# An attention and mixture-of-experts kernel: the second expert's rows turned in two halves, and the router's search step issued in two parts

## The chip, the cores and the metric

The kernel runs on one core of a Trainium2 chip. A core has five engines that run their own instruction queues in order: TensorE (PE, with its weight loads shown as PEld), VectorE (DVE), ScalarE (ACT), GpSimd (POOL) and SyncE (SP, here used to start DMAs). The metric is the device time in microseconds (us) of one execution.

## What is computed

Attention with a sigmoid in place of the softmax, for 8 batches and 12 heads of 448 positions and 64 columns; its result, as 3584 rows of 768 columns, goes through a mixture of 8 experts, each of which takes 448 rows:

```
scores = scale * q @ k.T - log(S)
attn = 1 / (1 + exp(-scores))
x = (attn @ v), heads side by side          # (3584, 768)
logits = x @ w_gate                          # (3584, 8)
for idx in argsort(-logits.flatten()):       # best pair of token and expert first
    tok, e = idx // E, idx % E
    if assigned[tok] >= 0 or counts[e] >= cap: continue
    assigned[tok] = e; counts[e] += 1
for e in range(E):
    h = maximum(x[assigned == e] @ w1[e], 0)
    out[assigned == e] = h @ w2[e]
```

All inputs and the output are float32. An expert's sequence of work follows from the order in which experts fill up.

## The kernel before

**Attention** runs first, pair of heads by pair of heads, and stores the rows to a scratch tensor (xs). The change does not touch it.

**The experts** follow, in the order in which they fill up, kx = 0 to 7. What the text calls expert 1 is the one with kx = 1, the second. In each, first products (`moe`, L718 to L739) give hidden columns in four groups of 256, then second products (L752 to L777) give output columns in three groups of 256. Each float32 matrix is split into a high and a low part (wh and wl, xh and xl, hh and hl), so a product is three matmuls: L734, L736, L738, then L771, L773, L775. The text calls each such matmul of 128x128 by 448 columns one product. There are 4 x 2 x 2 x 9 = 144 and 3 x 2 x 2 x 12 = 144 of them in an expert, 288 in all. Expert 0 does its first group in two cuts of 256 and 192 columns, which makes 324. The generator `moe` yields once per product.

**Rows of an expert.** Its 448 rows come in four blocks j of 128, 128, 128 and 64. `gather` (L623) fetches one block from xs with an indirect DMA on POOL's queue. `xturn` (L628) turns one half hf (384 of 768 columns) of a block: three transposes on PE into a bank of PSUM (L639), from which ACT writes xh (L642) and DVE writes xl (L643). So an expert needs eight of these turnings. The bank is one of two named tp, or, for `wide` and the second half, half of one of two tiles named sc. The sc tiles also take the sums of the products. The first products read the half hf = 0 (dd = 0 to 2) in their first 18 products of a group and hf = 1 in the next 18.

**Turning back.** `untranspose` (L648) turns an expert's output back, on PE (L652) through a tp bank and ACT (L657), and after the third group `scatter` sends a block of rows out on POOL's queue.

**Weights.** `stream` loads the weights (wr, on SP's queue, after the expert's number r_ei has been read) and splits them three and two units ahead: ACT writes wh (L603), POOL writes wl (L605).

**The router** finds the next expert and its rows. It is a generator (`phase`, L324). For each expert from 1 to 6 it does `keys`, a search of 16 steps, `pick`, `place` and `lists`, and ends with the list of rows, r_idx (L298). A step of the search counts on DVE how many keys lie over three thresholds (L178, three passes), and then, for every expert but the first, sums the counts and sets the next thresholds on DVE too (L194 to L217). `yield T_...` hands back a planned cost in ns.

**The order** of all this is written out by the loop at L816 to L858, instruction for instruction: the schedule is manual, and each engine takes its instructions in that order. The loop keeps a clock of planned time. Each product adds 189 ns (107 in expert 0's first group). At each product it may issue the next part of the router, if the clock has reached the time set by the previous part, and one of the `chores`: a list of jobs with due times, of which the first one due is taken, not more than one in 1000 ns:

```
if t >= t_route:
    t_route = t + next(route, 0) + SLACK
...
if t >= t_chore:
    c = next((c for c in chores if c[0] <= t), None)
    if c:
        ...
        t_chore = t + CHORE_NS
```

`prepare` (L820) is called when the list of the next expert is there: it makes the gathers and the eight turnings of that expert chores (for expert 1 the gathers are issued at once), the turnings due 5000 to 14000 ns later. `flush` (L833), at an expert's end, issues whatever chores the next expert cannot do without. Ahead of the first product the router is run through expert 0's list, and then by one part more (EARLY).

Of the kernel before, what the change touches and what calls it, by code (L numbers as in the profile page):

```python
# [26 lines left out]
YT_BUFS = 3  # L27
LATE_PER_STEP = 3
LATE_KEYS = 7
T_KEYS, T_KE, T_STEP, T_DVE, T_KAP, T_PICK, T_TOT, T_OH, T_BT = 3600, 2100, 2050, 2025, 500, 2600, 600, 3800, 600  # L30
SLACK = 150
CHORE_NS = 1000
H_POOL = 8
# [10 lines left out]
def _s32(v):  # L44
    v &= 0xFFFFFFFF
    return v - (1 << 32) if v >= (1 << 31) else v
# [72 lines left out]
class Router:  # L119
# [42 lines left out]
    def search(self, pe):  # L162

        nc, K, wk, KT = self.nc, self.K, self.wk, self.KT
        p = self.bank()
        for g in range(2):
            nc.tensor.transpose(p[:, g * 112:(g + 1) * 112],
                                KT[:, g].rearrange("p e c -> p (e c)"), K.ident[:112, :112])
        KE = wk.tile([128, 224], F32, name="r_KE")
        nc.vector.tensor_copy(KE, p[:, :224])  # L170
        T, JP = K.c0, None
        X = None if pe else self.bank().bitcast(I32)
        for st in range(16):
            sh = 30 - 2 * st
            cnt = wk.tile([128, 3], BF, name="r_cnt") if pe else K.CN
            for i in range(3):
                junk = wk.tile([128, 224], BF, name="r_junk")
                nc.vector.tensor_scalar(junk, KE, T[:, i:i + 1].bitcast(F32), None, OP.is_ge, OP.add,  # L178
                                        accum_out=cnt[:, i:i + 1])
            nX = None  # L180
            if 0 < st < 15:
                nX = wk.tile([128, 3], I32, name="r_X") if pe else X[:, 4 * (st % 2):4 * (st % 2) + 3]
            acc = wk.tile([128, 1], F32, name="r_acc")
            j2 = wk.tile([128, 3], F32, name="r_j2")
            if pe:
                if nX is not None:
                    nc.vector.tensor_scalar(nX, K.kk[:, st + 1], JP, None, OP.bitwise_xor)
                yield T_STEP
                pc = self.bank()
                nc.tensor.matmul(pc[:, :3], K.G, cnt, start=True, stop=True)  # L190
                tot = pc[:, :3]
            else:
                ct = wk.tile([128, 32], F32, name="r_ct")
                nc.vector.transpose(ct, cnt)  # L194
                if nX is not None:
                    nc.vector.tensor_scalar(nX, K.kk[:, st + 1], JP, None, OP.bitwise_xor)
                s2 = wk.tile([128, 2], F32, name="r_s2")
                nc.vector.tensor_reduce(s2, ct.rearrange("p (e r) -> p e r", r=16), AX.X, OP.add)
                ct2 = wk.tile([128, 32], F32, name="r_ct")
                nc.vector.transpose(ct2.rearrange("p (e r) -> p e r", r=16), s2[:, :, None].to_broadcast([128, 2, 16]))  # L200
                tot = ct2[:, :3]
            nc.vector.tensor_scalar(j2, tot, 447.5, TWO23, OP.is_ge, OP.add, accum_out=acc)
            nJ = wk.tile([128, 1], I32, name="r_J")
            if st == 0:
                J = wk.tile([128, 1], I32, name="r_J0")
                nc.vector.tensor_scalar(J, acc.bitcast(I32), sh, None, OP.logical_shift_left)
                PF = wk.tile([128, 1], I32, name="r_PF")
                nc.vector.tensor_scalar(PF, J, 31, -1, OP.arith_shift_right, OP.bitwise_xor)
                nc.vector.tensor_scalar(nJ, PF, _s32(0x80000000), J, OP.bitwise_or, OP.bitwise_xor)
                T = wk.tile([128, 3], I32, name="r_T")  # L210
                nc.vector.tensor_scalar(T, K.kk[:, 1], nJ, None, OP.bitwise_xor)
            else:
                if st < 15:
                    T = wk.tile([128, 3], I32, name="r_T")
                    nc.vector.scalar_tensor_tensor(T, acc.bitcast(I32).to_broadcast([128, 3]), sh, nX,
                                                   OP.logical_shift_left, OP.bitwise_xor)
                nc.vector.tensor_scalar(nJ, acc.bitcast(I32), sh, JP, OP.logical_shift_left, OP.bitwise_xor)  # L217
            JP = nJ
            if not pe:
                yield T_DVE  # L220
        kap = wk.tile([128, 1], I32, name="r_kap")
        nc.vector.tensor_scalar(kap, JP, K.gfin, None, OP.bitwise_xor)
        self.kap = kap.bitcast(F32)
# [116 lines left out]
def moe_attention(tc, q, k, v, w_gate, w1, w2, out):  # L340
# [7 lines left out]
    with contextlib.ExitStack() as ctx:  # L348
# [270 lines left out]
        def blocks():  # L619
            for j in range(4):  # L620
                yield j, min(128, S - 128 * j)

        def gather(kx, j, n):  # L623
            t = xg[kx, j] = xp.tile([128, DM], F32, name="xr", bufs=XR_BUFS)
            nc.gpsimd.indirect_dma_start(out=t[:n], out_offset=None, in_=xs,  # L625
                                         in_offset=bass.IndirectOffsetOnAxis(ap=listed[kx][:n, j:j + 1], axis=0))

        def xturn(kx, j, n, hf, wide):  # L628
            if (j, hf) == (0, 0):
                XH[kx] = (xp.tile([128, ND, S], F32R, name="xh", bufs=2),  # L630
                          xp.tile([128, ND, S], F32R, name="xl", bufs=2))
            xh, xl = XH[kx]
            if wide and hf:
                p = ps_s.tile([128, 2, 512], F32, name="sc")[:, 0]
            else:
                p = ps_t.tile([128, 512], F32, name="tp")
            for i in range(3):
                dd = hf * 3 + i
                nc.tensor.transpose(p[:, i * n:(i + 1) * n], xg[kx, j][:n, dd * 128:(dd + 1) * 128], ident[:n, :n])  # L639
            pv = p[:, :3 * n].rearrange("p (a t) -> p a t", a=3)  # L640
            sl = (slice(None), slice(hf * 3, hf * 3 + 3), slice(j * 128, j * 128 + n))
            nc.scalar.activation(xh[sl], pv, AF.Copy)  # L642
            nc.vector.tensor_tensor(xl[sl], pv, xh[sl].bitcast(F32), OP.subtract)  # L643

        scat, chores = [], []
        MM = 189

        def untranspose(kx, yr, i, yt, j, n, t0=0, end=False):  # L648
# [167 lines left out]
        for kx in range(E):  # L816
            turned = kx + 1 == E
            start = clock[0]

            def prepare():  # L820
                t0 = clock[0]
                lag = max(5000, min(14000, start + 40000 - t0))
                for j, n in blocks():
                    if kx:
                        chores.append((t0 + 1500 * j, kx + 1, lambda j=j, n=n: gather(kx + 1, j, n)))
                    else:
                        gather(1, j, n)
                for j, n in blocks():
                    for hf in range(2):
                        chores.append((t0 + lag + 1500 * j, kx + 1,  # L830
                                       lambda j=j, n=n, hf=hf: xturn(kx + 1, j, n, hf, False)))

            def flush(kx):  # L833
                for c in [c for c in chores if c[1] <= kx]:
                    chores.remove(c)
                    c[2]()

            for step, cost in enumerate(moe(kx)):
                clock[0] += cost
                t = clock[0]  # L840
                if kx == 0 and step == 35:
                    flush(0)
                if t >= t_route:
                    t_route = t + next(route, 0) + SLACK
                if not turned and kx + 1 in listed:
                    prepare()
                    turned = True
# [3 lines that stand above are left out]
                        chores.remove(c)  # L851
                        c[2]()
                        t_chore = t + CHORE_NS
            if not turned:
                while kx + 1 not in listed:
                    next(route)
                prepare()
            flush(kx + 1)  # L858
# [28 lines left out]
```

## Time and profile before

| | us |
|---|---|
| median of 3 runs | 883.03 (881.66 to 885.39) |
| the profiled execution | 883.43 |
| its span, first to last instruction | 881.7 |
| PE busy within the span | 840.1 |
| DVE busy | 542.4 |
| first product of expert 0 | at 332.80 |
| first product of expert 1 | at 405.83 |
| first product of expert 2 | at 475.69 |

Rows of the profile read like this. In a timeline: start, duration, engine, line of the kernel, operation, output and input tiles by name, shape, count, and in brackets how long the engine was idle before and for whom it waited. In a table of windows: the window, its length, then the busy time of each engine asked for (with the number of instructions), the clock that was granted to PE as a share of full speed, the busy share of the DMA engines, and GB/s. A matmul's recorded duration reaches into the next one's, since matmuls are pipelined; the distance of starts is what one costs.

### The profile page before, as it was taken

The numbers are of one execution on the slowest core, as the hardware profiler recorded it, in microseconds if no ns is written. First come the engines' busy times: TensorE is split into PE (matmuls) and PEld (weight loads), VectorE is DVE, ScalarE is ACT, GpSimd is POOL, SyncE is SP. The second block draws the span as 40 slices with busy tenths as digits, with TensorE's granted clock in tenths as the row PEclk, the third lists the DMA queues.
The fourth block names the chain that finished last, engine by engine and source line by source line (L and its number), as shares of the span: only waits on it lengthen the run. The fifth ranks groups of instructions, "written<-read, shape, count | busy, mean of one in ns | idle before, by whom it ended". The sixth has DMA issues, their size and how long they took to land.

```text
span 881.7 us, 16211 instructions
## 1 busy us (share of the span) xinstructions
PE 840.1 (95%) x5467; PEld 636.9 (72%) x5467; DVE 542.4 (62%) x2060; ACT 447.3 (51%) x612; POOL 466.0 (53%) x446
## 2 busy tenths in 40 slices
PE   6999999999999739998999999999999999999996
PEld 3455555555554528987988988988888888999996
DVE  4566555555554988958859879779779631332130
ACT  6777677777775734434434434534434344541420
POOL 9744344444410014854864873873883883851561
PEclk9999999999999979998999999999999999999999
DMA  9866766666621855443442442551542542634643
GB/s 173 165 142 149 153 126 127 127 126 127 126 43 54 270 192 154 120 138 123 128 136 97 160 155 81 177 162 57 189 153 72 170 153 90 209 96 141 203 151 126
DMA packets 213811, 122.16 MB, mean 139 GB/s; under 512 B 153344, under 2 KB 202496, under 8 KB 213728
## 3 DMA queue, kind: packets, MB, share of 16 engines
q1 hardware_dynamic: 200992, 87.62, 38.2%
q0 software_dynamic: 10880, 33.28, 12.0%
q8 instruction: 43, 0.70, 0.3%
q10 hardware_dynamic: 1856, 0.23, 0.2%
q14 instruction: 40, 0.33, 0.1%
HBM read 96.76 MB, written 24.31 MB: 137 GB/s over the span
## 4 chain that ended last, share of the span: by engine, by line
PE 82%; DVE 11%; issue 2%; DMA 2%; POOL 1%; SPq 1%; ACT 1%; POOLq 0%; DVEq 0%; ACTq 0%
PE tp L457 13%; PE sc L433 11%; PE sc L736 9%; PE sc L734 9%; PE sc L738 9%; PE sc L773 6%; PE sc L775 6%; PE sc L771 6%; DVE r_junk L178 4%; PE tp L463 2%; PE sc L443 2%; PE tp L639 2%; PE tp L652 2%; PE tp L478 1%; PE rt L289 1%
## 5 line engine op out<-in xcount | busy, mean ns | idle before, releaser
L605 POOL TENSOR_TENSOR wl<-wr,wh 128x768 fp32r<-128x768 f32 (+1 forms) x96 | 204.9, 2145 | 124.5 <-ACT wh L603 116.8
L423 ACT ACTIVATE at<-sc,bias 128x896 f32<-128x896 f32 x168 | 161.5, 1006 | 67.1 <-PE sc L443 38.4
L383 POOL DMA_DIRECT2D nkq<-in_q_dram x188 | 118.4, 646 | 116.2 <-DVE kqT L408 104.6
L775 PE MATMUL sc<-hh,wl 128*128 128x448 f32 (+2 forms) x400 | 150.2, 375 | 0.0
L738 PE MATMUL sc<-xh,wl 128*128 128x448 f32 (+2 forms) x396 | 146.2, 369 | 0.0
L736 PE MATMUL sc<-xl,wh 128*128 128x448 f32 (+2 forms) x396 | 146.0, 369 | 0.1
L773 PE MATMUL sc<-hl,wh 128*128 128x448 f32 (+2 forms) x400 | 145.5, 364 | 0.2 <-POOL hl L746 0.2
L734 PE MATMUL sc<-xh,wh 128*128 128x448 f32 (+2 forms) x396 | 145.0, 366 | 0.0
L771 PE MATMUL sc<-hh,wh 128*128 128x448 f32 (+2 forms) x400 | 144.1, 360 | 0.4 <-issue 0.4
L178 DVE TENSOR_SCALAR_CACHE_REDUCE r_junk<-r_KE,r_T 128x224 bf16<-128x224 f32 x315 | 123.2, 441 | 0.1
L603 ACT ACTIVATE wh<-wr 128x768 fp32r<-128x768 f32 (+1 forms) x112 | 102.0, 939 | 36.3 <-DMA wr<-in_moe_w_dram 23.4
L457 PE MATMUL tp<-at,nv 128*64 128x448 f32 x576 | 118.8, 548 | 0.0
L746 POOL TENSOR_TENSOR hl<-yt,hh 128x896 fp32r<-128x896 f32 x32 | 68.4, 2136 | 48.8 <-ACT yt L745 47.2
L742 ACT ACTIVATE hh<-sc 128x896 fp32r<-128x896 f32 x32 | 29.5, 921 | 117.1 <-PE sc L738 117.1
L417 DVE TENSOR_TENSOR kqL<-kqT,kqH 128x896 fp32r<-128x896 f32 (+1 forms) x49 | 52.5, 1073 | 58.5 <-ACT kqH L416 58.4
L773 PEld LDWEIGHTS sc<-hl,wh 128*128 128x128 f32 x400 | 75.8, 189 | 6.8 <-issue 1.1
L625 POOL DMA_INDIRECT xr<-xs,r_idx x32 | 32.0, 999 | 91.2 <-ACT wh L603 80.2
L736 PEld LDWEIGHTS sc<-xl,wh 128*128 128x128 f32 x396 | 75.2, 190 | 6.7 <-issue 0.5
L457 PEld LDWEIGHTS tp<-at,nv 128*64 128x64 f32 x576 | 37.1, 136 | 59.1 <-issue 56.6
L734 PEld LDWEIGHTS sc<-xh,wh 128*128 128x128 f32 x396 | 75.2, 190 | 6.0
L771 PEld LDWEIGHTS sc<-hh,wh 128*128 128x128 f32 x400 | 76.0, 190 | 4.8 <-issue 0.6
L738 PEld LDWEIGHTS sc<-xh,wl 128*128 128x128 f32 x396 | 75.1, 190 | 5.3
(166 smaller groups left out, 1266.1 us busy)
## 6 DMA issues: line engine op xcount, KB each, us to landing
wr<-in_moe_w_dram SPq DMA_DIRECT2D x64, 384.0 KB, 3.0
wr<-in_moe_w_dram SPq DMA_DIRECT2D x48, 512.0 KB, 3.6
nkq<-in_k_dram SPq DMA_DIRECT2D x192, 56.0 KB, 2.6
xs<-xr SPq DMA_DIRECT2D x32, 336.0 KB, 3.3
nkq<-in_q_dram POOLq DMA_DIRECT2D x188, 56.0 KB, 2.7
nv<-in_v_dram SPq DMA_DIRECT2D x92, 96.0 KB, 2.7
ys<-yt SPq DMA_DIRECT2D x20, 112.0 KB, 1.9
nr<-in_v_dram SPq DMA_DIRECT2D x46, 32.0 KB, 2.2
```

The costliest lines, as they stand in the source:

```text
L178: nc.vector.tensor_scalar(junk, KE, T[:, i:i + 1].bitcast(F32), None, OP.is_ge, OP.add, accum_out=cnt[:, i:i + 1])
L383: qn.dma_start(t[o:o + 32, n], rws[x])
L423: nc.scalar.activation(a, p[:, :, :S], AF.Sigmoid, bias=bias, scale=1 / math.sqrt(D))
L457: nc.tensor.matmul(p[j * 64:j * 64 + 64, :S], nat["v", b, g][:, h0 + j, c, :], AT[b, pr, c][:, j, :], start=(c == 0), stop=(c == 2 and pr ...
L603: nc.scalar.activation(hi, raw[u], AF.Copy)
L605: eng.tensor_tensor(lo, raw[u], hi.bitcast(F32), OP.subtract)
L734: nc.tensor.matmul(ph[:, f, lo:hi], wh[:, a, fs], xh[:, dd, lo:hi], start=st, stop=False)
L736: nc.tensor.matmul(ph[:, f, lo:hi], wh[:, a, fs], xl[:, dd, lo:hi], start=False, stop=False)
L738: nc.tensor.matmul(ph[:, f, lo:hi], wl[:, a, fs], xh[:, dd, lo:hi], start=False, stop=en)
L771: nc.tensor.matmul(py[:, d2, :w], wh[:, a, dsl], h1, start=st, stop=False)
L773: nc.tensor.matmul(py[:, d2, :w], wh[:, a, dsl], h2, start=False, stop=False)
L775: nc.tensor.matmul(py[:, d2, :w], wl[:, a, dsl], h1, start=False, stop=(j == 1 and a == 3))
```

## The change

The turnings of expert 1 are given out differently. Only the four first halves (hf = 0) become chores, due 1500 ns apart as before. The four second halves go to a list, `second`, and are issued after products 2, 6, 10 and 14 of expert 1 itself (counted from 0), in place of whatever else the loop would have issued there. The second halves of blocks 1 and 3 use an sc tile in place of a tp bank. Experts 2 to 7 keep their eight chores.

A step of the router's search for experts 1 to 6 is now handed out in two parts, the counts (T_CNT, 1000 ns) and the sums with the new thresholds (T_SUM, 875 ns), where it was one part (T_DVE, 2025 ns). The instructions of a step and their order stay the same.

```diff
-T_KEYS, T_KE, T_STEP, T_DVE, T_KAP, T_PICK, T_TOT, T_OH, T_BT = 3600, 2100, 2050, 2025, 500, 2600, 600, 3800, 600
+T_KEYS, T_KE, T_STEP, T_CNT, T_SUM, T_KAP, T_PICK, T_TOT, T_OH, T_BT = 3600, 2100, 2050, 1000, 875, 500, 2600, 600, 3800, 600
 SLACK = 150
...
                 yield T_STEP
+            else:
+                yield T_CNT
+            if pe:
                 pc = self.bank()
...
             if not pe:
-                yield T_DVE
+                yield T_SUM
...
-        scat, chores = [], []
+        scat, chores, second = [], [], []
...
+                if not kx:
+                    for j, n in blocks():
+                        chores.append((t0 + lag + 1500 * j, 1, lambda j=j, n=n: xturn(1, j, n, 0, False)))
+                        second.append(lambda j=j, n=n: xturn(1, j, n, 1, j % 2))
+                    return
                 for j, n in blocks():
                     for hf in range(2):
...
                 if kx == 0 and step == 35:
                     flush(0)
+                if kx == 1 and step % 4 == 2 and second:
+                    second.pop(0)()
+                    continue
                 if t >= t_route:
```

## The prediction

> **What bounds the kernel now.** I read the page first: engines, the 40 slices, the chain that ended last.
>
> ```profile
> PE 840.1 (95%) x5467; PEld 636.9 (72%) x5467; DVE 542.4 (62%) x2060; ACT 447.3 (51%) x612; POOL 466.0 (53%) x446
> PEclk9999999999999979998999999999999999999999
> PE 82%; DVE 11%; issue 2%; DMA 2%; POOL 1%; SPq 1%; ACT 1%; POOLq 0%; DVEq 0%; ACTq 0%
> ```
>
> TensorE sets the end: 82% of the chain is its own work. The granted clock has two dents, in slices 15 and 19, around 330 and 410 us. The second lies where expert 0 ends and expert 1 begins. Next I read the table of windows, cut at the first products of an expert, and then PE's timeline where expert 0 ends.
>
> ```profile
> 406.00:475.60 69.60, 68.66 (x368) 60.36 (x368) 56.14 (x293) 27.19 (x41) 45.26 (x30) 0.96 0.41 131
> ...
> 590.00:650.00 60.00, 59.69 (x341) 52.27 (x339) 48.37 (x254) 27.49 (x44) 39.35 (x26) 1.00 0.42 132
> ```
>
> Within the experts PE (first busy column) is busy for 59.69 of 60 us. Whatever is moved there can gain only what little idle there is; it can cost wherever PE is made to wait.
>
> ```profile
> 396.40 0.49 PE L639 MATMUL tp<-ident,xr 128*128 128x128 f32 x3
> ...
> 399.50 0.49 PE L639 MATMUL tp<-ident,xr 128*128 128x128 f32 x3
> ...
> 400.44 0.36 PE L775 MATMUL sc<-hh,wl 128*128 128x448 f32 x1
> 401.88 1.01 PE L639 MATMUL tp<-ident,xr 128*128 128x128 f32 x6 [1.08 <-DVE xl L643]
> 403.60 0.87 PE L639 MATMUL tp<-ident,xr 128*128 128x128 f32 x6 [0.71 <-DVE xl L643]
> 405.32 0.58 PE L639 MATMUL tp<-ident,xr 64*128 64x64 f32 x3 [0.85 <-DVE xl L643]
> 405.83 0.74 PE L734 MATMUL sc<-xh,wh 128*128 128x448 f32 x1
> ...
> 411.27 0.38 PE L736 MATMUL sc<-xl,wh 128*128 128x448 f32 x1
> 411.49 0.38 PE L652 MATMUL tp<-ident,yt 128*128 128x128 f32 x2
> 411.63 0.45 PE L738 MATMUL sc<-xh,wl 128*128 128x448 f32 x1
> 411.92 0.36 PE L734 MATMUL sc<-xh,wh 128*128 128x448 f32 x1
> ```
>
> Three of expert 1's eight turnings (xturn; 396.40 is the first, 399.50 the third) run among expert 0's products, five at its end. I call E the end of an expert's products: here 400.65 (the last starts at 400.44; products stand 0.20 apart, rows below). The first product comes at E+5.2, because tp has two buffers, each released by DVE's xl, so pairs of turnings follow each other by 403.60 - 401.88 = 1.72 us. Then comes the clock:
>
> ```profile
> 404.00:406.00 2.00, 1.15 (x9) 0.61 0.00 0
> 406.00:408.00 2.00, 2.00 (x6) 0.50 0.01 4
> ...
> 410.00:412.00 2.00, 2.00 (x9) 0.68 0.67 236
> ```
>
> It is 0.50 until about 411.2. From 405.83 to 411.27 thirteen products and one turning back (untranspose, L652) ran. One of those costs 0.22 (411.27 to 411.92 is 0.65, less two products). So 5.4 us stand in place of 13 x 0.20 + 0.22 = 2.9, a loss of **2.5 us**. This boundary is what the change aims at; at the most some 6 us are to be had.
>
> **The planner first.** The second edit decides more than the first. A part of the router is issued at the first product whose clock has reached the previous one plus cost plus SLACK, and a product counts 189 ns. A search step was 2025 + 150 = 2175, 12 products (2268). Now its first part is 1000 + 150 = 1150, which 6 products (1134) miss by 16 ns: 7; its second 875 + 150 = 1025: 6. That is **13 for 12**, sixteen times per expert. All of a round in products (3750, 16 steps, 650, 2750, 750, 3950, 750, 150 ns): 20 + 192 + 4 + 15 + 4 + 21 + 4 + 1 = 261 before, 277 after, against 288 in an expert (324 in expert 0, 72 of them at 107 ns). Stepping the clock through expert 0 gives its list for expert 1 at product 280 of 324 before and 299 after (fifteen steps at one product more, less two in the 107 ns part, where a step takes 21 either way, and 6 for the half step that EARLY no longer covers). Each next list is 261 or 277 products on, less an expert's: for experts 2 to 6 at 217, 190, 163, 136, 109 of 288 before; **252, 241, 230, 219, 208** after. Turnings are due 5000 ns (27 products) or more behind the list, and chores are issued every 6 products, older ones (untranspose) ahead. So:
>
> - into expert 1: before, three turned inside and five at the end (as the rows show); after, all four first halves at the end, four second halves at products 2, 6, 10, 14;
> - into 2: before one at the end; after the gathers are at 271, 277, 283 and the end, and **all eight** turnings at the end;
> - into 3: before none; after gathers at 241, 271, 277, 283 and **all eight** at the end;
> - into 4: four at the end; into 5 and 6: one each; into 7: none, as before.
>
> The trace bears the clock out for the kernel before: one L639 at the end of expert 1, and expert 2's all inside:
>
> ```profile
> 475.36 0.40 PE L639 MATMUL tp<-ident,xr 64*128 64x64 f32 x3
> 475.69 0.47 PE L734 MATMUL sc<-xh,wh 128*128 128x448 f32 x1
> ```
>
> ```profile
> L639 PE MATMUL tp<-ident,xr x24: 221/272/329, 526.3 to 538.8; 128*128 128x128 f32 x18, 64*128 64x64 f32 x6
> ```
>
> **Prices.** A turning among products:
>
> ```profile
> 525.85 0.36 PE L775 MATMUL sc<-hh,wl 128*128 128x448 f32 x1
> 526.05 0.37 PE L771 MATMUL sc<-hh,wh 128*128 128x448 f32 x1
> 526.26 0.49 PE L639 MATMUL tp<-ident,xr 128*128 128x128 f32 x3
> 526.51 0.45 PE L773 MATMUL sc<-hl,wh 128*128 128x448 f32 x1
> 526.80 0.37 PE L775 MATMUL sc<-hh,wl 128*128 128x448 f32 x1
> ```
>
> From 526.05 to 526.80 two products took 0.75 in place of 0.41 (one alone: 526.05 - 525.85): 0.34 each. At an end, the queues count:
>
> ```profile
> 400.84 0.91 ACT L791 COPY yt<-sc 128x896 f32<-128x896 f32 x1 [0.32 <-PE sc L775]
> 402.46 0.95 ACT L642 ACTIVATE xh<-tp 128x384 fp32r<-128x384 f32 x2 [0.72 <-PE tp L639]
> ```
>
> ```profile
> 391.15 0.98 POOL L625 DMA_INDIRECT xr<-xs,r_idx  x1
> ...
> 394.94 0.91 POOL L625 DMA_INDIRECT xr<-xs,r_idx  x1 [0.30 <-issue]
> ...
> 468.32 1.83 POOL L605 TENSOR_TENSOR wl<-wr,wh 128x768 fp32r<-128x768 f32 x1 [1.73 <-ACT wh L603]
> ```
>
> ```profile
> DMA to landing us min/median/max: 3.8/4.3/4.8
> ```
>
> ACT has the yt copy ahead of the first xh, until E+1.1. PE runs in the written order, so every product of the next expert queues behind the flushed turnings. Gathers go 1.26 us apart (391.15 to 394.94 is three of them) and land 4.3 after issue (the answer on tile xr). On POOL those behind product 264 wait for that product's split (L605).
>
> **Into expert 1.**
>
> ```profile
> 389.83 0.16 DVE L298 TENSOR_SCALAR r_idx<-rt 128x4 int32<-128x4 f32 x1 [0.93 <-PE rt L296]
> ```
>
> Idx came at 389.99; 19 products later is about 394.0. E moves to 399.6 (three turnings less). The gathers start at 394.1 and the last lands at 394.1 + 3.8 + 4.3 = 402.2, E+2.6. Expert 1's first weights hang on r_ei, equally late:
>
> ```profile
> 380.40 0.13 DVE L249 TENSOR_SCALAR r_ei<-r_c 1x1 int32<-1x1 f32 x1
> ```
>
> ```profile
> 381.37 16.75 SPq L592 DMA_DIRECT2D wr<-in_moe_w_dram  x6
> ```
>
> ```profile
> DMA to landing us min/median/max: 4.2/4.2/4.2
> ```
>
> ```profile
> 388.24 0.86 ACT L603 ACTIVATE wh<-wr 128x768 fp32r<-128x768 f32 x1
> ```
>
> Before, they landed at 385.6 for use at 388.24; 3.9 later is 1.3 too late, for which ACT, then POOL's split and the gathers wait; there is room to 392.3, so no price. The second pair starts when the first is released, E+2.2; its xh are done some 1.45 later (402.46 + 0.95 less 401.88 is 1.53, the last block smaller): first product at E+3.7 in place of E+5.2, **-1.5**. Inside: -3 x 0.34, and +4 second halves, 0.5 each because the clock is low there: **+1.0**. The low clock stays (PE is as idle as before). They issue no DMA, only PE, ACT and DVE work, and hide as far as xl goes: product 18 reads them first, four products behind the last. The odd ones take the free sc buffer, which the yt copy releases at E+1.1. Together -0.5 (between -6, if the clock stays up too, and +2, if they are late for product 18).
>
> **Into expert 2.** POOL's split at 468.32 is followed by the gathers: 470.3, 471.6, 472.8, 474.1; they land at 474.6 to 478.4. E moves from 475.36 to about 473.2 (seven turnings, 2.4, and a stall of 0.66 less; four turnings back, 0.9, more, which the old kernel does a little later). First pair at 474.7, E+1.5, then 3 x 1.72, then the xh of block 3 about 0.7 later: first product at E+7.4 against E+0.33. Less seven turnings inside (2.4) and this stall:
>
> ```profile
> 468.86 0.55 PE L639 MATMUL tp<-ident,xr 128*128 128x128 f32 x3 [0.66 <-DVE xl L643]
> ```
>
> 7.4 - 0.3 - 2.4 - 0.7 = 4.0. The clock: PE turns for some 2 of 7.4 us, less than where it fell before, so again 2.5 lost (bounds 0 and 3.5): **+6.5**.
>
> **Into expert 3.** Gathers are no longer the limit (the last lands at E+4.3); pairs at E+0.1, 2.2, 3.9, 5.7, first product at E+6.4. Less 8 x 0.34 and 0.9 of waits on xl inside (below): +2.8, and the clock 2.5: **+5.3**. **Into 4:** two pairs, E+3.3, less 4 x 0.34: +1.9; for the clock 1.5, since so short a stretch may straddle what the gate looks at (between 0 and 2.5): **+3.4**. **Into 5 and 6:** 0.3 each, as at 475.36: **+0.6**.
>
> Splitting the search steps also halves what xl waits behind on DVE. PE's waits on it, experts only:
>
> ```profile
> PE tp L639 <- DVE xl L643: 4.2, 5, 1.1
> ```
>
> Of 4.2 us, 2.6 stand at expert 0's end and 0.7 at 468.86; 0.9 is left, in expert 2, and counted. For the split itself I take nothing: DVE's work in sum is unchanged, and DVE is idle 38% of the span.
>
> **Sum:** -0.5 + 6.5 + 5.3 + 3.4 + 0.6 = **+15.3**. The profiled execution took 883.4 (span 881.7), 0.4 above the median of the runs, 883.0: 898.7 or 898.3, so 898.5.
>
> [...] The gate cost 2.5 us where PE's longest idle piece was 1.08 us. [...]
>
> **Rivals.**
> 1. *Stalls without the low clock* at the three later boundaries: 15.3 - 6.5 = +8.8, **892**. For it: short gaps; against it: 404 to 411 us. [...] 0.17.
> 2. *Low clock for longer, later gathers*: the low stretch lasted some 6.8 us before (404.4, by the 0.61, to 411.2), of which turnings took the first; if products take all of it, about 1 us more each time, and if the gathers land at 4.8 behind a later split, 1 to 3 more: +6, **905**. 0.16.
> 3. *Faster:* the planner's slip not reaching the ends. If both parts of a step took 6 products, lists would stand where they stood or earlier, three first halves would be turned inside expert 0, and expert 1 would begin at E+1 with the clock up: 4.2 + 2.5 less about 1.5 for the moved halves, -5, **878**. It decides at 1134 ns for the first part; 1150 is over it, which speaks against it. 0.03.
> 4. *The edit does nothing:* lists later, but turnings still inside, because DVE and POOL run ahead. PE keeps the written order, so it waits behind whatever is flushed; 0.04, **883**.
>
> **How the numbers follow.** Forecast as reckoned, 894 to 903: 0.60, 898.5. With rivals 1 and 2 the range is 889.5 to 907.5. 0.5% (4.4 us) is about what a measurement can tell from no change. Slower by more: 0.60 + 0.17 + 0.16 = 0.93; within 0.04; faster 0.03.
>
> **What would show it.** In the profile after: search counts (L178) thirteen products apart; L639 in unbroken runs of four, eight, eight and four turnings at the ends; PE waits on xl and on gathered xr at the second and third end; granted clock 0.5 there. Were the lists at the old products, or PE busy through expert 1's end, the prediction is wrong at its root; were the clock at 1.0 there, by 6.5 us.

## The result, and the profile after

The changed kernel takes 905.0 us (median of 6 runs, 903.4 to 906.6), the kernel before 882.7 us beside it: a ratio of 1.0249, 95% interval 1.0227 to 1.0270. It is 22 us slower. The forecast was 898.5 us, within 889.5 to 907.5.

First the page of the changed kernel: engines, granted clock in 40 slices, and the chain that ended last.

```profile
PE 848.2 (94%) x5467; PEld 644.7 (71%) x5467; DVE 540.6 (60%) x2060; ACT 447.1 (50%) x612; POOL 462.7 (51%) x446
PEclk9999999999999969999997998999999999899999
PE 81%; DVE 7%; DMA 4%; issue 4%; POOL 2%; ACT 1%; SPq 1%; POOLq 0%; DVEq 0%; ACTq 0%
```

The counts of instructions are the old ones; the work has not changed, only when it is done. The dent in the clock at the end of expert 0 (slice 19 before, 18 in the new span) is gone, and dents have come in slices 22, 25 and 35: at the ends of experts 1 and 2 and within expert 6. Transfers have doubled their share of the chain, from 2% to 4%.

The next table is worked out from the timelines of PE in both profiled executions. A stretch goes from the first product of an expert to the first of the next, for expert 7 to its last product.

| stretch of expert | before, us | after, us | difference | forecast for its end | turnings at its end, before / after |
|---|---|---|---|---|---|
| 0 | 73.0 | 71.3 | -1.7 | -0.5 | 5 / 4 |
| 1 | 69.9 | 76.1 | +6.2 | +6.5 | 1 / 8 |
| 2 | 68.7 | 73.7 | +4.9 | +5.3 | 0 / 8 |
| 3 | 68.1 | 69.9 | +1.8 | +3.4 | 0 / 4 |
| 4 | 67.8 | 68.7 | +1.0 | +0.3 | 0 / 1 |
| 5 | 69.5 | 68.8 | -0.7 | +0.3 | 0 / 1 |
| 6 | 62.4 | 71.8 | **+9.4** | 0 | 0 / 0 |
| 7 | 61.6 | 61.1 | -0.5 | 0 | |

Before rounding the differences add up to 20.5 us; the spans differ by 902.0 - 881.7 = 20.3. The column of the forecast does not match a stretch term by term: what the low clock costs behind an end falls into the next stretch. So part of the agreement at expert 1 is luck, since within its +6.2 stands a gain of 2.7 us: the old low clock at its start is gone, while the forecast had it stay. Cut at product 50 of each expert instead, behind these spells, the differences for the ends of experts 0 to 5 are -2.4, +7.6, +4.1, +3.6, -0.5 and -0.5 us, and expert 6 itself comes to +8.2.

Now PE's timeline of the changed kernel where experts 0, 1, 2 and 3 end, and within expert 6. L642 is the transposes of a turning (three matmuls each), L737 a first product; both lines stand three lower than before.

```profile
400.24 0.49 PE L642 MATMUL tp<-ident,xr 128*128 128x128 f32 x3
401.15 0.52 PE L642 MATMUL tp<-ident,xr 128*128 128x128 f32 x3 [0.42 <-DMA xr<-xs,r_idx]
402.56 0.85 PE L642 MATMUL tp<-ident,xr 128*128 128x128 f32 x6 [0.89 <-DMA xr<-xs,r_idx]
403.88 0.47 PE L737 MATMUL sc<-xh,wh 128*128 128x448 f32 x1 [0.47 <-ACT xh L645]
...
472.99 0.84 PE L642 MATMUL tp<-ident,xr 128*128 128x128 f32 x6 [2.69 <-issue]
474.68 1.54 PE L642 MATMUL tp<-ident,xr 128*128 128x128 f32 x6 [0.84 <-DVE xl L646]
476.75 1.54 PE L642 MATMUL tp<-ident,xr 128*128 128x128 f32 x6 [0.53 <-DVE xl L646]
478.82 1.22 PE L642 MATMUL tp<-ident,xr 64*128 64x64 f32 x6 [0.53 <-DVE xl L646]
479.98 0.74 PE L737 MATMUL sc<-xh,wh 128*128 128x448 f32 x1
...
546.04 0.82 PE L642 MATMUL tp<-ident,xr 128*128 128x128 f32 x6
548.18 1.01 PE L642 MATMUL tp<-ident,xr 128*128 128x128 f32 x6 [1.32 <-DVE xl L646]
550.44 1.51 PE L642 MATMUL tp<-ident,xr 128*128 128x128 f32 x6 [1.25 <-DVE xl L646]
552.49 1.22 PE L642 MATMUL tp<-ident,xr 64*128 64x64 f32 x6 [0.53 <-DVE xl L646]
553.63 0.74 PE L737 MATMUL sc<-xh,wh 128*128 128x448 f32 x1
...
620.54 1.18 PE L642 MATMUL tp<-ident,xr 128*128 128x128 f32 x6
622.73 0.86 PE L642 MATMUL tp<-ident,xr 64*128 64x64 f32 x6 [1.02 <-DVE xl L646]
623.55 0.47 PE L737 MATMUL sc<-xh,wh 128*128 128x448 f32 x1
...
785.03 0.87 PE L642 MATMUL tp<-ident,xr 128*128 128x128 f32 x3 [6.47 <-DMA xr<-xs,r_idx]
```

Read by the counts: 4 turnings, then 8 (four rows of six matmuls), 8 and 4, each run unbroken by products. At the end of expert 1 PE stands for 2.7 us before the first of them; this row does not name what it waits for ("issue"), but in the second profile of the same kernel (e9, below) the like wait of 2.08 us is put down to the gathered rows. The first product comes 10.05 us after the last one of expert 1 (both counted by their starts). At the end of expert 2 it is 7.80, of expert 3 3.22. The last row is the one that the forecast did not have: in the middle of expert 6 PE stands for **6.47 us** because a block of expert 7's rows has not landed. What PE waited for, experts only, in the changed kernel (total, times, longest):

```profile
PE tp L642 <- DMA xr<-xs,r_idx: 7.8, 3, 6.5
PE tp L642 <- DVE xl L646: 6.5, 8, 1.3
PE tp L642 <- issue: 2.7, 1, 2.7
```

The granted clock at the four ends and within expert 6, from the table of windows of the changed kernel (window, length, PE's busy time with its count, granted clock, share of the DMA engines, GB/s):

```profile
404.00:406.00 2.00, 1.84 (x10) 1.00 0.10 28
...
474.00:476.00 2.00, 1.32 (x6) 0.66 0.14 40
476.00:478.00 2.00, 1.47 (x8) 0.50 0.00 0
...
484.00:486.00 2.00, 2.00 (x10) 0.78 0.65 197
```

```profile
548.00:550.00 2.00, 1.01 (x6) 0.93 0.35 109
...
556.00:558.00 2.00, 2.00 (x11) 0.86 0.07 10
```

```profile
624.00:626.00 2.00, 2.00 (x10) 0.70 0.00 0
626.00:628.00 2.00, 2.00 (x8) 0.50 0.12 32
628.00:630.00 2.00, 2.00 (x12) 0.94 0.48 165
```

```profile
786.00:788.00 2.00, 2.00 (x7) 0.50 0.23 70
788.00:790.00 2.00, 2.00 (x12) 0.84 0.34 84
```

Behind expert 0 the clock stays at 1.00, though PE waits for 1.8 of the 3.6 us from 400.24 to 403.88. Behind experts 1, 2 and 3 it falls to 0.50 for some time, and so it does behind the long wait within expert 6, which thereby costs more than its 6.47 us.

### The profile page after: what moved, and what is told of

It reads as the page before. It is cut to its first block, busy times and chain, and to the rows that moved or that the text cites. A ratio compares the mean times of both kernels' runs of the same rounds, so it can differ in the third digit from the quotient of the medians.

```text
span 902.0 us, 16214 instructions
## 1 busy us (share of the span) xinstructions
PE 848.2 (94%) x5467; PEld 644.7 (71%) x5467; DVE 540.6 (60%) x2060; ACT 447.1 (50%) x612; POOL 462.7 (51%) x446
## 4 chain that ended last, share of the span: by engine, by line
PE 81%; DVE 7%; DMA 4%; issue 4%; POOL 2%; ACT 1%; SPq 1%; POOLq 0%; DVEq 0%; ACTq 0%
PE tp L460 13%; PE sc L436 11%; PE sc L739 9%; PE sc L737 9%; PE sc L741 8%; PE sc L776 7%; PE sc L774 7%; PE sc L778 7%; DVE r_junk L178 2%; PE tp L466 2%; DMA xr<-xs,r_idx 2%; PE sc L446 2%; PE tp L642 2%; PE tp L655 1%; PE tp L481 1%
## 5 line engine op out<-in xcount | busy, mean ns | idle before, releaser
L608 POOL TENSOR_TENSOR wl<-wr,wh 128x768 fp32r<-128x768 f32 (+1 forms) x96 | 202.5, 2122 | 134.6 <-ACT wh L606 131.4
L739 PE MATMUL sc<-xl,wh 128*128 128x448 f32 (+2 forms) x396 | 148.3, 374 | 0.4 <-DVE xl L646 0.4
L778 PE MATMUL sc<-hh,wl 128*128 128x448 f32 (+2 forms) x400 | 148.1, 370 | 0.0
L737 PE MATMUL sc<-xh,wh 128*128 128x448 f32 (+2 forms) x396 | 146.7, 371 | 0.5 <-ACT xh L645 0.5
L737 PEld LDWEIGHTS sc<-xh,wh 128*128 128x128 f32 x396 | 76.7, 194 | 6.8 <-ACT xh L645 0.6
L778 PEld LDWEIGHTS sc<-hh,wl 128*128 128x128 f32 x400 | 75.9, 190 | 4.8 <-issue 0.2
```

The costliest lines, as they stand in the source:

```text
L608: eng.tensor_tensor(lo, raw[u], hi.bitcast(F32), OP.subtract)
L737: nc.tensor.matmul(ph[:, f, lo:hi], wh[:, a, fs], xh[:, dd, lo:hi], start=st, stop=False)
L739: nc.tensor.matmul(ph[:, f, lo:hi], wh[:, a, fs], xl[:, dd, lo:hi], start=False, stop=False)
L778: nc.tensor.matmul(py[:, d2, :w], wl[:, a, dsl], h1, start=False, stop=(j == 1 and a == 3))
```

## The experiments

The theory that came with the forecast is called **A**: the slip of the lists, 13 products for a step of the search in place of 12, moves turnings to the ends, and that is the loss; the moved second halves by themselves gain. Rivals: **B**, the second halves cost by themselves; **C**, handing a step to VectorE in two parts costs by itself. (A fourth, **D**, on expert 7's gathers, comes with e5; **E** and **F** come with e6 and e9.) Each kernel was timed beside the kernel before on the same chip.

| run | time, us | before beside it | ratio, 95% interval |
|---|---|---|---|
| e1: both edits, 12 products | 881.9 | 883.6 | 0.9982 (0.9965 to 0.9999) |
| e2: second halves alone | 882.2 | 883.6 | 0.9982 (0.9967 to 0.9996) |
| e3: two parts alone, 13 products | 905.4 | 883.6 | 1.0246 (1.0217 to 1.0276) |
| e4: neither, but 13 products | 907.4 | 883.6 | 1.0269 (1.0238 to 1.0300) |
| e5: the change, expert 7's gathers first | 895.0 | 882.8 | 1.0117 (1.0083 to 1.0151) |
| e6: both, 12 products, EARLY = 2 | 877.7 | 882.8 | 0.9937 (0.9919 to 0.9956) |
| e7: both, 11 products, EARLY = 2 | 882.7 | 882.8 | 0.9997 (0.9987 to 1.0008) |
| e8: as e7 without second halves | 885.6 | 882.8 | 1.0036 (1.0024 to 1.0049) |

### e1: 980 for 1000

```diff
-... T_CNT, T_SUM, ... = ... 1000, 875, ...
+... T_CNT, T_SUM, ... = ... 980, 875, ...
```

> The changed kernel with 980 in place of 1000 ns for the first part of a search step, so that a step takes 6 + 6 = 12 products as in the kernel before. Theory A (late lists): the lists come at 286 of 324 and 223, 196, 169, 142, 115 of 288; two turnings are left at the end of expert 0, two at the end of expert 1, none later, and the gathers of expert 7 are back at products 0 to 43. Time 876 to 880, faster than before. Theory B (the moved second halves cost by themselves): 883 to 890. Theory C (handing a step to VectorE in two parts costs by itself, whatever the lists do): 895 to 905.

Twenty nanoseconds of a planned cost take back the whole loss: 881.9. C falls. The size of the gain was overrated by every theory that expected one: -0.2%, just clear of no change.

### e2: the first edit alone

The kernel before with the list `second` and its turnings after products 2, 6, 10 and 14, and T_DVE as it was.

> The kernel before with the first edit alone (second halves of expert 1 at products 2, 6, 10, 14), search steps in one part. Theory A: lists as before, one turning left at the end of expert 0, gap there about 0.8 us in place of 5.4, clock at 1.0; 875 to 879. Theory B: 883 to 890. Theory C: as A.

It gains 0.2%, so B falls as a loss, but A's 875 to 879 was missed. The timelines of PE and of DVE in e2 show what ate the gain:

```profile
409.75 0.48 PE L736 MATMUL sc<-xl,wh 128*128 128x448 f32 x1 [1.39 <-DVE xl L643]
```

```profile
407.02 0.44 DVE L178 TENSOR_SCALAR_CACHE_REDUCE r_junk<-r_KE,r_T 128x224 bf16<-128x224 f32 x1
...
409.22 0.21 DVE L217 TENSOR_SCALAR r_J<-r_acc,r_J 128x1 int32<-128x1 int32 x1
409.35 0.35 DVE L643 TENSOR_TENSOR xl<-sc,xh 128x192 fp32r<-128x192 f32 x1
```

The xl of the last second half stands behind a whole step of the search, from 407.02 to 409.43, and the first product that reads it (L736, product 19) makes PE wait 1.39 us. In the changed kernel, with the step in two parts, PE waits 0.26 us at that product:

```profile
410.65 0.47 PE L739 MATMUL sc<-xl,wh 128*128 128x448 f32 x1 [0.26 <-DVE xl L646]
```

Besides, two turnings, not one, stand behind the last product of expert 0: the one due at product 323 is issued after it. The gap there is 2.6 us, not 0.8.

### e3: the second edit alone

```diff
-                if not kx:
-                    for j, n in blocks():
-                        chores.append((t0 + lag + 1500 * j, 1, lambda j=j, n=n: xturn(1, j, n, 0, False)))
-                        second.append(lambda j=j, n=n: xturn(1, j, n, 1, j % 2))
-                    return
```

> The changed kernel with the second edit alone (search steps in two parts of 7 and 6 products), all eight turnings of expert 1 as chores. Theory A: all eight of expert 1's turnings at the end of expert 0, the rest as in the changed kernel; 906 to 911, slower than the changed kernel. Theory B: about 883. Theory C: 900 to 911.

905.4, as the changed kernel: with late lists the first edit is worth nothing that can be measured. A had it at 906 to 911, above the changed kernel, and missed. The gap at the end of expert 0 is 6.6 us with eight turnings against 3.8 with four, and its stretch 2.9 us longer; but the stretches of experts 1 and 2 come out 0.8 and 1.9 shorter in e3's profile, where the clock fell later at the end of expert 2.

### e4: neither edit, 13 products

```diff
-T_KEYS, T_KE, T_STEP, T_DVE, ... = 3600, 2100, 2050, 2025, ...
+T_KEYS, T_KE, T_STEP, T_DVE, ... = 3600, 2100, 2050, 2200, ...
```

> The kernel before with 2200 in place of 2025 ns for a search step: one part, no halves, but 13 products for a step. Theory A: seven, eight, four, three, one and one turnings at the ends of experts 0 to 5, and the gathers of expert 7 at products 49 to 67 of expert 6; 900 to 906. Theory B and theory C: 881 to 885.

907.4: a step in one part, no second halves, and the loss is the whole 2.7%. With e1 this settles it: **the thirteenth product is the cause**, and no part of what the two edits were about. The turnings at the ends are 7, 8, 4, 3, 1 and 1, as A had them; the time lies 1.4 us over A's 900 to 906. Its expert 6 takes 71.4 us, as in the changed kernel; that belongs to the slip too.

### e5: expert 7's gathers ahead of the backlog

POOL's timeline of the changed kernel within expert 6 (L693 scatters, L628 gathers), and the answer on tile xr from 764 to 792 us for the time from issue to landing:

```profile
776.68 0.99 POOL L693 DMA_INDIRECT out_dram<-xr,r_idx  x1 [0.16 <-issue]
...
777.98 0.91 POOL L693 DMA_INDIRECT out_dram<-xr,r_idx  x1 [0.21 <-issue]
779.19 0.98 POOL L628 DMA_INDIRECT xr<-xs,r_idx  x1 [0.30 <-issue]
...
783.00 0.90 POOL L628 DMA_INDIRECT xr<-xs,r_idx  x1 [0.30 <-issue]
```

```profile
DMA to landing us min/median/max: 4.6/5.6/6.6
```

Only two transfers of that stretch have a landing in the trace: 6.6 us is the scatter at 776.68, 4.6 the last gather, of 64 rows. The gathers come at 779 to 783 us, the first turning wants its rows at 778.6 (785.03 less 6.47). By the planner's clock the lists being late leaves eight untransposes of expert 5 for expert 6 in place of four; they stand ahead of the gathers in the list of chores, which puts these at products 49 to 67, while the turnings keep their own due time, product 75. The experiment puts the four gathers at the head of the list, for expert 7 alone:

```diff
-                        chores.append((t0 + 1500 * j, kx + 1, lambda j=j, n=n: gather(kx + 1, j, n)))
+                        chores.insert(j if kx == E - 2 else len(chores),
+                                      (t0 + 1500 * j, kx + 1, lambda j=j, n=n: gather(kx + 1, j, n)))
```

> The changed kernel, but the four gathers of expert 7 go ahead of the untransposes that are waiting as chores, so that they are issued at products 1, 13, 19 and 25 of expert 6 in place of 49, 55, 61 and 67. Theory D (the late gathers are the whole of the 9.4 us that expert 6 took longer): expert 6 takes 62 to 63 us from first product to first product, time 894 to 897. Rival (the rows arrive late whatever the order, since POOL has scatters and splits ahead and other transfers run): 68 to 72 us there, 901 to 906.

POOL's timeline of e5, first and last gather:

```profile
764.06 1.53 POOL L628 DMA_INDIRECT xr<-xs,r_idx  x1
...
768.39 0.91 POOL L628 DMA_INDIRECT xr<-xs,r_idx  x1 [0.30 <-issue]
```

They are 15 us earlier, expert 6 takes 63.5 us in place of 71.8, and the time falls from 905.0 to 895.0. Theory D holds: the late gathers of expert 7 were some ten of the 22 us by the times, 8.4 by the stretch of expert 6 (71.83 less 63.47), which stays 0.5 over D's 62 to 63. The two figures need not agree to a microsecond, since the clock differs between executions: in e5's profile it did not fall behind expert 3.

### e6: both edits at 12 products, lists where they were

```diff
-T_... = 3600, 2100, 2050, 1000, 875, ...
+T_... = 3600, 2100, 2050, 980, 875, ...
-EARLY = 1
+EARLY = 2
```

> Both edits with 980 and 875 ns (6 + 6 products) and EARLY = 2, so that the whole first step is ahead of the products as in the kernel before: lists, gathers and turnings stand where the first edit alone has them (e2), and the two parts are the only difference. Theory E (the parts let xl in between, so the second halves are ready for their readers): PE's wait on xl at expert 1's products 18 to 20 falls from 1.4 to 0.2 or 0.3 us, time about 1 us under e2's, 880 to 882. Rival (the parts do nothing): the wait stays, as e2.

**877.7 us, 0.6% under the kernel before**: the fastest of all the versions. It beats e2 by more than expected, by 4 us by the ratios and by 1.9 between the two profiles. PE and DVE where e2 lost 1.39 us, now in e6:

```profile
410.36 0.48 PE L739 MATMUL sc<-xl,wh 128*128 128x448 f32 x1 [0.36 <-DVE xl L646]
```

```profile
409.96 0.35 DVE L646 TENSOR_TENSOR xl<-sc,xh 128x192 fp32r<-128x192 f32 x1
410.23 0.20 DVE L197 STREAM_TRANSPOSE r_ct<-c_CN 128x32 f32<-128x32 f32 x1
```

The xl runs between the two parts of a step. Over the experts e2's PE waits for xl 1.39 us at the product and 2.7 at turnings; e6 waits for xl 0.7 at products and not at all at turnings, though at the end of expert 0 a wait of 1.28 us for ACT's xh has come instead. So, with the lists in the same places, the second edit is what makes the first pay, when its planned costs add up to the old number of products. What it gives without the second halves at 12 products was not run.

### e7 and e8: 11 products

980 and 790 ns (6 + 5 products) and EARLY = 2; e8 also without the first edit.

> Both edits with 980 and 790 ns (6 + 5 = 11 products) and EARLY = 2. Theory A: lists at 266 of 324, 189, 146, 103, 60, 17 of 288; all turnings but expert 1's second halves run among products, no end has any, gaps of 0.2 us and the clock at 1.0 everywhere; 876 to 880. Rival (11 products are 2.2 us, about what VectorE takes for a step, so it falls behind and PE waits for xl, r_KT and r_kap): 883 to 890.

> As e7, without the first edit: eight turnings of expert 1 as chores, five among expert 0's products and three at its end. Theory A: gap of 3 to 4 us there, with or without a spell of half clock; 2 to 4 us over e7. If the halves are worth nothing once the lists are early: as e7.

In e7 no end has a turning left and every gap is 0.2 or 0.3 us, as expected, and yet it takes 882.7, as the kernel before, above theory A's range and 0.3 under the rival's. The waits of PE in e7:

```profile
PE tp L642 <- DVE xl L646: 2.6, 2, 2.3
PE rt L292 <- DVE r_oh L287: 1.0, 2, 0.5
PE rt L167 <- DVE r_KT L158: 0.9, 3, 0.3
PE rt L232 <- DVE r_kap L225: 0.7, 2, 0.4
```

That is 5.2 us of waiting for VectorE, against 0.6 + 0.3 for the same kinds (r_KT, r_oh) and 0.7 for xl in e6. VectorE's share of the chain is 18% in e7 and 7% in e6. So the rival's mechanism is there: 11 products are too few for a step. In the traces of e7 and of the kernel before, the counts of successive steps start 2.33 us apart in most of a search, with VectorE busy for 22.6 of 24 us in such a stretch of the kernel before (412 to 436 us); 11 products of 0.204 us are 2.24 us, 12 are 2.45. Where the rest of the 5 us between e6 and e7 goes was not followed up. e8 is 2.8 us over e7, as theory A had it, so the second halves seem to be worth something when lists are early. How much is not shown: up to product 50 of expert 1 the two profiles differ by 1.3 us, and then the clock fell in e8 within expert 1 (to 0.50 at 461.4 us, for 3.4 us), behind a wait of 2.6 us that in e7 was 2.3 and left the clock up.

### Two executions more

The clock at the ends did not follow the length of the gaps: in the changed kernel 3.8 us at the end of expert 0 left it at 1.00, and 3.22 at the end of expert 3 did not. So two kernels were profiled once more.

> The changed kernel once more, for one profile. In the first profile the clock stayed at 1.00 at the end of expert 0 (a gap of 3.8 us) and fell to 0.50 at the ends of experts 1, 2 and 3. Theory F (what decides is how the gap falls on periods of the gate that run on their own): the gaps come out the same within 0.3 us where no transfer is late, but the stretch at 0.50 differs in start and length by some us, and an end may change sides. Rival (the gap's own pattern of work decides): clock rows as in the first profile, end by end.

> The same for the kernel with 13 products for a step in one part (e4), where a gap of 6.6 us at the end of expert 0 left the clock at 1.00. Theory F: in another execution it may well fall to 0.50 there, by a gap of the same length and work. Rival: 1.00 again.

The changed kernel took 901.2 us in that one run, e4 910.4. In e9 the same gap at the end of expert 3, PE's timeline and the windows:

```profile
620.20 0.86 PE L642 MATMUL tp<-ident,xr 64*128 64x64 f32 x6 [1.02 <-DVE xl L646]
621.01 0.47 PE L737 MATMUL sc<-xh,wh 128*128 128x448 f32 x1
```

```profile
622.00:624.00 2.00, 2.00 (x13) 1.00 0.00 0
624.00:626.00 2.00, 2.00 (x14) 1.00 0.36 94
626.00:628.00 2.00, 2.00 (x13) 1.00 0.29 103
```

The same four turnings, the same wait of 1.02, a gap of 3.21 us against 3.22: in the first execution the clock fell, here it stayed at 1.00. In e4 the gap of 6.62 us at the end of expert 0 left it at 1.00; in e10 it fell in that gap, which grew to 7.30. Theory F's forecast for the clock came true in both pairs of executions, the rival's in neither. That gaps without a late transfer come out the same within 0.3 us did not hold at the end of expert 2: 6.60 us in e9 for 7.80, because in the first profile the clock fell within that gap and in e9 behind it (at 550.91, the first product being at 550.82). At the end of expert 1 it is 8.39 for 10.05, for the same reason and because its first turning stands 0.6 sooner behind the last product.

## Why the prediction was right, and where it was not

- **The planner's slip** was right to the count: 13 for 12, and 4, 8, 8, 4, 1, 1 and 0 turnings at the ends. e4 shows that the slip alone is enough, e1 that its removal is enough to take the whole loss back.
- **The lengths of the stalls** were near. First product behind E (0.2 less than the gaps above): forecast 3.7, 7.4, 6.4, 3.3; measured 3.6, 9.9, 7.6, 3.0. Two were too short. At the end of expert 1 the first pair came at E+2.9 rather than E+1.5, and pairs that fell under the low clock went 2.07 us apart (476.75 - 474.68) rather than 1.72; at the end of expert 2 the low clock came into the gap as well. In e9, with the clock at 1.00 in both, pairs go 1.72 apart and the first products come 8.2 and 6.4 behind E.
- **"into 7: none, as before"** was the step that failed. The turnings were counted, and they do stand where they stood; the gathers that feed them were not followed, so their price was put at nothing. Expert 6 took 9.4 us longer in the profile, 6.47 of them a single wait for these rows, and moving the gathers ahead brought 8.4 of them back, 10 by the times of e5.
- **The low clock as a price of 2.5 us for an end** was mis-sized, and its kind was wrong: whether it comes changed from one execution of a kernel to the next. At the end of expert 0 "the low clock stays" did not come true in either profile of the changed kernel, at the end of expert 3 in one of two. The forecast had 2.5 + 2.5 + 1.5 = 6.5 for three ends and kept the old 2.5 at the first. The 1.5 for expert 3's end was the author's estimate; the runs show 1.7 there in one execution and nothing in the other. In the first profile the half clock took 2.4, 1.5 and 1.7 us from the products behind the three ends and about 1.1 and 1.2 more within the first two gaps, 7.9 together; in e9 it took 1.7, 1.7 and nothing.
- **"For the split itself I take nothing"** was wrong. From e2 to e6 it takes some 1.0 of 1.39 us of waiting away at one product and the waits of turnings for xl; e6 against e2 gives -0.6% against -0.2%. The changed kernel has the gain at that product too (0.26 us left), and it is drowned.
- The sum of +15.3 thus met 22.3 with a gap that is more than covered by the one term left out. Without it, e5 stands 12.2 us over the kernel before: the terms that were reckoned came out 3 us too high together. The time as reckoned was given as 894 to 903, and 905.0 is over that; it is the figure of the rival "low clock for longer, later gathers", but that rival's 6 us were to come from the ends, whereas 8 to 10 us came from expert 6, of which it did not speak: that its number fits is luck. That the measured time lay in the range owes as much to the rival "later gathers" having been given room as to the reckoning.
- **The rival "stalls without the low clock"** described a thing that happens, at some ends in some executions, but the short gaps named for it do not explain it: in the first profile the clock fell at the end of expert 3, where no idle piece was longer than 1.02 us, and in e9 the same pieces left it at 1.00.
- **Of the signs**, "search counts thirteen products apart" did not show. In both profiles the counts of successive steps start 2.33 us apart in most of a search, because VectorE does not wait for PE within it and runs ahead (from 412 to 436 us no row of VectorE names PE in either); what the planner's clock moves is PE's part of the router around a search, and with it the list. And of the two ends named for waits on gathered rows only the first has one.

## What to carry to other kernels

Where a planner compares a clock that moves in steps with planned costs, the costs are rounded up to the step: reckon every part in steps before and after an edit that cuts a job in two, since 16 ns of overhang here became 3 us in each round and 22 us in the end. When a list or a flag comes later, follow everything that hangs on it through every queue that it shares, the transfers that feed the moved work first; the largest loss stood in an expert that had no turning out of place. And an edit that measures as next to nothing can need another one: the second halves alone gave 0.2%, with the split steps at 12 products and the old places of the lists 0.6%. Before a part is called useless, then, it is worth trying beside the other with the schedule held in place.

## What the runs showed of the hardware that was not expected

The time at half clock comes in one size. A row of two microseconds with the clock c holds 2 x (1 - c) / 0.5 us at half clock. By the rows above, with those left out at 0.50: behind expert 3 it is 1.2 + 2 + 0.24 = 3.4 us, behind expert 2 0.28 + 3 x 2 + 0.56 = 6.8, behind expert 1 1.36 + 4 x 2 + 0.88 = 10.2, and in the kernel before, by the rows in the prediction, 1.56 + 2 x 2 + 1.28 = 6.8. These are one, two and three times 3.4 us, and so are the eleven spells at the ends in e4, e5, e9 and e10, by their windows of 1 us: 3.4 four times, 6.8 four times and 10.2 three times. The places where the clock falls show the same step. In the changed kernel these are 474.63, 549.72, 624.81 and 781.83 us, which are 22, 22 and 46 times 3.413 us apart. The steps are not tied to the kernel: in e9 the falls at the ends of experts 1 and 2 stand at 479.23 and 550.91 us, 21 times 3.413 apart, but 4.60 and 1.19 us behind those of the first profile, which is a third of a step off in both cases (1.35 and 0.35 steps). So the same gap lay differently against the steps in the two executions; at the end of expert 3 the clock fell in the first and stayed up in the second.

Cut into such steps, the traces of the changed kernel and of the kernel before also show what stood around the falls. In the 3.41 us ahead of the four falls just named PE was busy for 0.84, 1.56, 2.32 and 0.15 us, by the profile's busy time, and for 1.86 ahead of the fall at 404.45 us in the kernel before. In the changed kernel it was busy for 2.10 of the 3.41 us from 399.54 to 402.95, at the end of expert 0, and the clock stayed at 1.00. So less work did not always bring a fall, and what decides stays open. All five spells ended with the first step in which PE was busy without a break (3.41 of 3.41 us); in the steps of these spells ahead of that one it was busy for 0.21 to 2.83 us.
